# One lasting tile for P1's sums and the results, and ScalarE's last stores behind its last copy, in a convolution and hardswish kernel

## The chip, the cores and the metric

The kernel runs on one core of one Trainium2 chip. Its engines are TensorE (PE in the profile; its weight loads, which overlap the matmuls, are PEld), VectorE (DVE), ScalarE (ACT), GpSimd (POOL) and SyncE (SP), which here only issues transfers. The metric is the device time of one execution in microseconds (us). Beside a run's time the profile has its span, the time from the first to the last instruction of the program.

## The reference

Each head of a lightweight convolution has a softmax over seven taps; the result goes through a feed-forward layer with a hardswish. Cut to what matters:

```python
w = exp(weight - max); w = w / (sum(w) + 1e-9)        # weight [8, 7]
attn[b, s] = sum_k w[head, k] * x_padded[b, s + k]     # x [8, 4096, 192], causal, 24 channels a head
x = attn.reshape(32768, 192)
h = x @ w_in                                           # w_in [192, 2048]
g = h * clip(h + 3.0, 0.0, 6.0) / 6.0
return g @ w_out                                       # w_out [2048, 192], float32
```

## The kernel before

The 32768 tokens are worked through in 32 blocks of 1024 (two groups of N = 512 tokens). Tokens lie along the free dimension, and the 2048 hidden units are 2 x 8 chunks of 128 partitions (`NP` = 8). The first block is computed in a plain way (`out_direct`). Blocks 1 to 31 each go through `first_layer` and `second_layer`. The whole order of instructions is written out by hand: the program is traced under `tc.manual_schedule()`, and each engine runs its instructions in that order. The Tile layer adds the waits that the data need.

**First layer** (`first_layer`). It runs 16 steps, n = 0 to 15. Each step has 18 matmuls (L508) in parts of high and low precision into two PSUM banks, a scaling on ScalarE (L520), the clipped factor on ScalarE (`relu`, L302) and its product with h on VectorE (`gate`, L306), which writes two quarters of the tile `g`. Only after the gate are the banks free for a later step, so a late gate makes TensorE wait. Between the steps stand jobs: before step 0 the results left over from the block before and one tap of the next block's convolution, and after steps 1, 5 and 9 one more tap each (`conv_jobs`, L986, VectorE, 128 x 1536 values, both inputs in SBUF).

Behind each odd step below 8 GpSimd forms **P1's sums** for one pair of chunks: `small_sums` (L575) makes four sums or differences of quarters of A11 and writes them into the tile `s1`, pairs (0, 1), (2, 3), (4, 5), (6, 7) behind steps 1, 3, 5 and 7. Behind the odd steps above 8 it forms S3 (`g_sums`, L412) and issues a transfer that adds A22 onto A21 in place (L556).

**Second layer** (`second_layer`). `g @ w_out` is done by seven products of 2 x 2 blocks (`prod`), a part of each again by seven products of half size (`small`, `level_two`). Matmuls (L616) come in four streams side by side, each with a cost and a due time; `do(t, ...)` puts other engines' work between them. The small products of product 1 read `s1` and are done by clock 32; `tiles` at clock 33 then takes a new tile of results. Its eight chunks of 512 values have these uses:

| chunk | before | after |
|---|---|---|
| 0, 1, 2 | p7, p5, u3 | the same |
| 3 | transposed results on their way out | free in most blocks; fourth buffer in the last |
| 4, 5 | transposed results | the same |
| 6 | p2, and c12 in the last block | the same |
| 7 | fourth buffer in the last block | transposed results |

`store` (L462 and `store_rows`, L372) takes the next chunk from the list `xts`, transposes a result of 96 x 512 values into it on VectorE, and issues three transfers to `out`, one for each 32 rows, on SyncE unless other queues are named. A block has four stores: p7, p2, then u3 and p5, which are finished (`finish`, L837 and the adds at L456) in the next block before step 0.

**The tile's reuse.** `s1` and `results` are tiles of the same pool, one buffer and one tag (`shared`), so they take turns in the same memory. The first instruction that writes a new one waits until everything that read or wrote the old one is done, the transfers to `out` among them. It stands between steps 1 and 2:

```python
if n == 1:
    s1.append(ot.tile([P, NP, N], F32, name="s1", tag="shared")[:])
if n < NP and n % 2:
    small_sums(s1[-1], A11, (1, 2, 3, 4), nc.gpsimd, every[n - 1 : n + 1])
```

**The last block** finishes its own results. `end_lower` makes c12 and u3 for the lower 256 tokens and stores them, rows 0 and 2 of three issued by SyncE and row 1 by ScalarE (`both`). `end_upper` copies the last piece out of PSUM on ScalarE (L825), adds it to c12 on VectorE and to u3 on GpSimd (L827), transposes and stores the upper tokens, rows by SyncE and ScalarE again.

Of the kernel before, what the change touches and what calls it, by code (L numbers as in the profile page):

```python
# [11 lines left out]
F32 = mybir.dt.float32  # L12
# [13 lines left out]
def kernel(  # L26
# [8 lines left out]
    nc = tc.nc  # L35
    P = nc.NUM_PARTITIONS
# [6 lines left out]
    N = 512  # L43
# [11 lines left out]
    NP = NC // 2  # L55
# [8 lines left out]
    ot = ctx.enter_context(tc.tile_pool(name="ot", bufs=1))  # L64
# [55 lines left out]
    w_s = cst.tile([P, 3, 4, NP // 2, QS], F32, name="w_s")  # L120
# [153 lines left out]
    A11, A21, A12, A22 = (g4[:, :, j] for j in range(4))  # L274
# [26 lines left out]
    def relu(r6, h):  # L301
        nc.scalar.activation(r6, h, ACT.Relu, bias=half[:], scale=1.0 / 6.0)  # L302

    def gate(g_, h):

        nc.vector.scalar_tensor_tensor(  # L306
            out=g_, in0=g_, scalar=1.0, in1=h, op0=ALU.min, op1=ALU.mult
        )
# [46 lines left out]
    every = range(NP)  # L355

    results, xts = [], []

    def new_results():
        results[:] = [ot.tile([P, NP, N], F32, name="results", tag="shared")]  # L360
        xts[:] = range(3, 6)

    def next_xt():
        xts.append(xts.pop(0))
        return results[0][:, xts[-1]]

    new_results()

    def store_rows(i, k, q, xt, j, dma=nc.sync, tokens=slice(0, N)):

        t0 = i * TB + k * N
        dma.dma_start(  # L372
            out=out[t0 + tokens.start : t0 + tokens.stop, q * QS : (q + 1) * QS].rearrange("(t r) d -> r t d", r=QS),
            in_=xt[j * QS : (j + 1) * QS, tokens].rearrange("r (t d) -> r t d", d=QS),
        )
# [79 lines left out]
    def add(out, x, y, op=ALU.add):  # L455
        nc.vector.tensor_tensor(out=out, in0=x, in1=y, op=op)  # L456

    def store(i, c, k, half_, qs=range(NQ), queues=(nc.sync,), tokens=slice(0, N)):

        xt = next_xt()  # L460
        r = slice(qs[0] * QS, (qs[-1] + 1) * QS)
        nc.vector.transpose(out=xt[r, tokens], in_=c[r, tokens])  # L462
        for q in qs:
            store_rows(i, k, half_ * NQ + q, xt, q, queues[q % len(queues)], tokens)
# [5 lines left out]
    def r32(ap):  # L470
        return ap.bitcast(F32R)
# [13 lines left out]
        nc.scalar.mul(r32(mix), mix, -4096.0)  # L485

    free_slots = list(range(4))
    y_own, y_other, pools, s1 = [], [None], [], []

    def swap_parts(dma=nc.sync):  # L490
        y_other[0] = pools[0].tile([P, 3, K3, N], F32, name="y_other", tag="other")
# [4 lines left out]
    def first_layer(i, jobs):  # L496

        slots = {}

        def both(n):  # L500
            return psum[:, 2 * slots[n] : 2 * slots[n] + 2]

        def mms(n, part, start=False, stop=False):
            group, c = divmod(n, NP)
            for s in range(K3):
                for k in range(2):
                    r = slice(k * D2, (k + 1) * D2)
                    nc.tensor.matmul(  # L508
                        out=psum[:, 2 * slots[n] + k], lhsT=r32(w_in_parts[part][r, c, s]),
                        rhs=r32(y_other[0][r, part, s] if group else y_own[part][r, s]),  # L510
                        start=start and s == 0, stop=stop and s == K3 - 1,
                        skip_group_check=True,
                    )

        def begin(n):
            slots[n] = free_slots.pop(0)
            mms(n, HIGH, start=True)
            mms(n, LOW)
            if n + 1 < count:
                nc.scalar.mul(both(n), both(n), 4097.0)  # L520
            else:
                lower, upper = (psum[:, 2 * slots[n] + k] for k in range(2))
                nc.scalar.mul(lower, lower, 4097.0)
                nc.vector.tensor_scalar(
                    out=upper, in0=upper, scalar1=4097.0, scalar2=None, op0=ALU.mult
                )

        def end(n):
            group, c = divmod(n, NP)
            mms(n, MIX, stop=True)  # L530
            to = g4[:, c, 1:3] if group else g4[:, c, 0::3]
            relu(to, both(n))
            gate(to, both(n))
            free_slots.append(slots[n])

        count = 2 * NP
        begin(0)
        begin(1)
        for job in jobs.get(-1, ()):
            job()  # L540
        for n in range(count):
            if n == count - 3:
                begin(n + 2)
            end(n)
            if n < count - 3:
                begin(n + 2)
            for job in jobs.get(n, ()):
                job()
            if n == 1:
                s1.append(ot.tile([P, NP, N], F32, name="s1", tag="shared")[:])  # L550
            if n < NP and n % 2:
                small_sums(s1[-1], A11, (1, 2, 3, 4), nc.gpsimd, every[n - 1 : n + 1])
            if n > NP and n % 2:
                pair = slice(n - NP - 1, n - NP + 1)
                g_sums(nc.gpsimd if n + 3 < count else nc.vector, (3,), range(NP)[pair], 2)
                nc.gpsimd.dma_start(out=S1[:, pair], in_=A22[:, pair], accum_op=ALU.add)  # L556
# [7 lines left out]
    def small_sums(to, x, which, engine=nc.gpsimd, r=every):  # L564

        r = slice(r[0], r[-1] + 1)
        x11, x12, x21, x22 = four_parts(x[:, r])
        s1, s2, s3, s4 = four_parts(to[:, r])
        forms = {
            1: (s1, x21, x22, ALU.add), 2: (s2, s1, x11, ALU.subtract),  # L570
            3: (s3, x11, x21, ALU.subtract), 4: (s4, x12, s2, ALU.subtract),
        }
        for n in which:
            o, p, q, op = forms[n]
            engine.tensor_tensor(out=o, in0=p, in1=q, op=op)  # L575
# [10 lines left out]
    def second_layer(i, between):  # L586
# [4 lines left out]
        sums2, p1 = z[:, 0:NP], z[0:DH, NP]  # L591
        ends = [psum[:, 2 * free_slots[0] + k] for k in range(2)] if last else [b, b]
        s5 = A22
        copy = nc.scalar.copy
        m = slice(0, DH)
        lo, hi = halves
        both = nc.sync, nc.scalar
# [39 lines left out]
        def small(n, m_, out, start=False, j=3):  # L637

            x, w = prod[n]
            sums, ws = {  # L640
                1: (s1[-1], w_s[:, 0]), 5: (s5, w_s[:, 1]), 2: (sums2, w_s[:, 2]),
            }[n]
            x11, x12, x21, x22 = four_parts(x)
            z1, z2, z3, z4 = four_parts(sums)
            b11, b12, b21, b22 = (
                w_out[:, h::2, w, q * QS : (q + 1) * QS] for h in range(2) for q in range(2)
            )
            t1, t2, t3, t4 = (ws[:, k] for k in range(4))
            xm, wm = {
                1: (x11, b11), 2: (x12, b21), 3: (z4, b22), 4: (x22, t4),  # L650
                5: (z1, t1), 6: (z2, t2), 7: (z3, t3),
            }[m_]
            for u in range(NP // 2):
                put(j, 1, lambda u=u: matmul(
                    j, out, wm[:, u], xm[:, u], start and u == 0
                ))
# [9 lines left out]
        def tiles():  # L666
            new_results()
            if last:
                xts.insert(0, NP - 1)
            late.update(zip(("p7", "p5", "u3"), (results[0][m, n] for n in range(3))))  # L670
            late["p2"] = results[0][m, 6]

# [128 lines left out]
        def finish(k):  # L801
# [4 lines left out]
                add(p5, b[m], p5)  # L806
            store(i, u3 if k else p5, k, 1)

        def end_lower():
            p5, u3, c12 = late["p5"], late["u3"], results[0][m, 6]  # L810
            two = slice(0, 2 * QS)
            copy(out=p5[third, lo], in_=a[fourth, lo])
            copy(out=c12[third, hi], in_=b[third, hi])
            nc.gpsimd.tensor_tensor(out=u3[two, hi], in0=u3[two, hi], in1=p5[two, hi], op=ALU.add)
            add(c12[two, hi], b[two, hi], p5[two, hi])
            nc.gpsimd.tensor_tensor(out=u3[:, lo], in0=u3[:, lo], in1=p5[:, lo], op=ALU.add)
            store(i, u3, 1, 1, (0, 1), (nc.gpsimd,), hi)
            add(c12[:, lo], b[m, lo], p5[:, lo])
            add(c12[:, lo], ends[0][m, lo], c12[:, lo])
            store(i, c12, 0, 1, queues=both, tokens=lo)  # L820
            store(i, u3, 1, 1, queues=both, tokens=lo)

        def end_upper():
            p5, u3, c12 = late["p5"], late["u3"], results[0][m, 6]
            copy(out=p5[third, hi], in_=c[fourth, hi])  # L825
            add(c12[:, hi], ends[1][m, hi], c12[:, hi])
            nc.gpsimd.tensor_tensor(  # L827
                out=u3[third, hi], in0=u3[third, hi], in1=p5[third, hi], op=ALU.add
            )
            add(c12[third, hi], c[fourth, hi], c12[third, hi])  # L830
            store(i, c12, 0, 1, queues=both, tokens=hi)
            store(i, u3, 1, 1, (2,), (nc.scalar,), hi)
# [33 lines left out]
    with tc.manual_schedule():  # L866
# [82 lines left out]
        n = 3  # L949
# [137 lines left out]
```

## Time and profile before

| | |
|---|---|
| time, median of 3 runs | 2218.27 us (2216.13, 2218.27, 2218.99) |
| profiled execution | 2217.5 us, its span 2215.7 us |
| granted TensorE clock | 0.999 |
| bytes moved by transfers | 264.28 MB, mean 119 GB/s |
| from and to HBM | 31.72 MB read, 25.17 MB written |
| L575 on POOL, 128 x 256 (min / median / max) | 726 to 732 / 739 to 742 / 2251 to 2346 ns |
| L986 on DVE, 128 x 1536, in 186 taps | 1771 / 1814 / 2425 ns |
| transfers of results, issue to landing | 1.5 / 4.3 / 13.7 us |

The page gives busy times of the engines and the chain that ended last: from the last instruction back, at each step, to what released it. In the tables of waits a line has the waiting engine and line, what ended the wait, the sum of the waits in us, their number and the longest. In a timeline a line has the start in us from the span's start, the length, engine, line, operation, what is written and read, how many instructions were merged, and in brackets the idle time before it and what ended that. "ACTq" and "SPq" are the queues of ScalarE and SyncE, where transfers are issued. A busy TensorE is a modelled time, so the chain, not the busy share, tells where it waits.

### The profile page before, as it was taken

What the parts mean: (1) busy time and instruction counts of PE and PEld (TensorE: products, weight loads), DVE (VectorE), ACT (ScalarE), POOL (GpSimd) and SP (SyncE); (2) the same over time, 40 slices, a digit from 0 to 9 for tenths busy, and PEclk for the clock granted to TensorE, in tenths of its full rate; (3) what the DMA queues carried; (4) which work ended last, traced back from release to release, by engine and by line L of the source; (5) the groups of instructions that cost most, each with busy time, mean ns of one, the idle gap of its engine ahead of it and who ended that gap; (6) DMA issues with size and microseconds to landing.
All of it is one profiled execution on the core that took longest, in us unless ns stands there. A gap on an engine that the chain in (4) does not pass through costs nothing.

```text
span 2215.7 us, 53039 instructions
## 1 busy us (share of the span) xinstructions
PE 2208.0 (100%) x22364; PEld 1581.8 (71%) x22364; DVE 1900.8 (86%) x1766; ACT 1615.0 (73%) x2112; POOL 1021.9 (46%) x1029
## 2 busy tenths in 40 slices
PE   9999999999999999999999999999999999999998
PEld 5477777777777777777777777777777777777776
DVE  8888888888898888888888888888888888888876
ACT  7478776687766777767877668776677776687765
POOL 2454543554434555335454355453455543554434
PEclk9999999999999999999999999999999999999999
DMA  6265658656577556685665766666755667656575
GB/s 157 56 116 112 130 106 148 116 109 125 112 133 139 103 109 124 121 149 104 114 125 111 141 124 109 118 119 126 142 101 110 127 114 148 111 111 127 99 134 91
DMA packets 304190, 264.28 MB, mean 119 GB/s; under 512 B 210992, under 2 KB 216112, under 8 KB 303952
## 3 DMA queue, kind: packets, MB, share of 16 engines
q0 software_dynamic: 82240, 201.95, 48.5%
q1 hardware_dynamic: 220472, 58.67, 14.7%
q8 instruction: 175, 2.87, 0.5%
q14 instruction: 63, 0.52, 0.1%
q10 hardware_dynamic: 1240, 0.27, 0.1%
HBM read 31.72 MB, written 25.17 MB: 26 GB/s over the span
## 4 chain that ended last, share of the span: by engine, by line
PE 98%; ACT 1%; DVE 0%; DMA 0%; issue 0%; DVEq 0%; ACTq 0%
PE psum L616 48%; PE psum L508 45%; PE psum L296 2%; PE psum L341 2%; DMA s<-g 0%; PE psum L881 0%; ACT g L302 0%; PE psum L889 0%; ACT psum L520 0%; ACT s L678 0%; DVE g L306 0%; DVE y L986 0%; DVE results L456 0%; DVE results L462 0%; ACT results L791 0%
## 5 line engine op out<-in xcount | busy, mean ns | idle before, releaser
L616 PE MATMUL psum<-g,w_out 128*32 128x512 f32 (+1 forms) x6340 | 899.5, 525 | 0.0
L306 DVE SCALAR_TENSOR_TENSOR g<-g,psum 128x1024 f32<-128x1024 f32 (+1 forms) x528 | 616.5, 1183 | 181.8 <-ACT g L302 181.4
L302 ACT ACTIVATE g<-psum,half 128x1024 f32<-128x1024 f32 (+1 forms) x528 | 564.7, 1086 | 6.3 <-PE psum L508 5.5
L616 PEld LDWEIGHTS psum<-g,w_out 128*32 128x32 f32 x6340 | 389.5, 110 | 217.6 <-issue 102.8
L508 PE MATMUL psum<-y,w_in 64*128 64x512 f32 x4464 | 521.4, 388 | 0.0
L508 PE MATMUL psum<-y_other,w_in 64*128 64x512 f32 x4464 | 519.0, 387 | 0.1
L520 ACT ACTIVATE psum<-psum 128x1024 f32<-128x1024 f32 x465 | 469.0, 1009 | 53.7 <-PE psum L508 50.8
L616 PE MATMUL psum<-s,w_out 128*32 128x512 f32 (+1 forms) x3272 | 503.7, 570 | 0.1
L508 PEld LDWEIGHTS psum<-y,w_in 64*128 64x128 f32 x4464 | 413.5, 184 | 115.7 <-issue 26.0
L508 PEld LDWEIGHTS psum<-y_other,w_in 64*128 64x128 f32 x4464 | 416.9, 184 | 92.1 <-DVE g L306 4.9
L575 POOL TENSOR_TENSOR s<-g 128x256 f32<-128x256 f32 x248 | 228.9, 923 | 426.7 <-DMA out_dram<-results 422.6
L986 DVE SCALAR_TENSOR_TENSOR y<-x,c_sb,y 128x1536 f32<-128x1536 f32 x186 | 346.0, 1860 | 2.6 <-ACT y L984 1.3
L679 POOL DMA_DIRECT2D s<-g x124 | 148.5, 1202 | 335.5 <-ACT s L678 293.0
L616 PE MATMUL psum<-g,w_s 128*32 128x256 f32 x1488 | 285.5, 379 | 0.0
L616 PEld LDWEIGHTS psum<-s,w_out 128*32 128x32 f32 x3272 | 176.4, 110 | 60.1 <-issue 33.0
L556 POOL DMA_DIRECT2D g<-g x124 | 150.0, 1214 | 106.5 <-issue 63.7
L616 PEld LDWEIGHTS psum<-g,w_s 128*32 128x32 f32 x1488 | 159.2, 110 | 42.6
L613 ACT COPY psum<-psum 32x512 f32<-32x512 f32 x186 | 89.4, 481 | 112.7 <-PE psum L616 109.3
L616 PE MATMUL psum<-s,w_s 128*32 128x256 f32 x744 | 170.7, 379 | 0.0
L616 PE MATMUL psum<-z,w_s 128*32 128x256 f32 x744 | 170.6, 379 | 0.0
L412 POOL TENSOR_TENSOR s<-g 128x1024 f32<-128x1024 f32 x62 | 166.8, 2691 | 0.8 <-DVE g L306 0.8
L575 DVE TENSOR_TENSOR g<-g 128x1024 f32<-128x1024 f32 x124 | 146.3, 1221 | 11.7 <-PE psum L616 8.5
(109 smaller groups left out, 2144.4 us busy)
## 6 DMA issues: line engine op xcount, KB each, us to landing
y_other<-y POOLq DMA_DIRECT2D x180, 384.0 KB, 8.8
g<-g POOLq DMA_DIRECT2D x124, 512.0 KB, 5.9
s<-g POOLq DMA_DIRECT2D x124, 512.0 KB, 6.6
out_dram<-results SPq DMA_DIRECT2D x378, 64.0 KB, 4.3
x<-in_x_dram SPq DMA_DIRECT2D x53, 388.5 KB, 5.8
stage<-in_moe_w_in_dram SPq DMA_DIRECT2D x16, 192.0 KB, 4.5
stage<-in_moe_w_out_dram SPq DMA_DIRECT2D x8, 384.0 KB, 6.4
x<-in_x_dram SPq DMA_DIRECT2D x7, 384.0 KB, 4.7
```

The source lines that it names most:

```text
L296: nc.tensor.matmul(out=psum[:, b], lhsT=w[r], rhs=src, start=start, stop=stop, skip_group_check=onto,)
L302: nc.scalar.activation(r6, h, ACT.Relu, bias=half[:], scale=1.0 / 6.0)
L306: nc.vector.scalar_tensor_tensor(out=g_, in0=g_, scalar=1.0, in1=h, op0=ALU.min, op1=ALU.mult)
L412: engine.tensor_tensor(out=o[:, r], in0=a[:, r], in1=b[:, r], op=op)
L508: nc.tensor.matmul(out=psum[:, 2 * slots[n] + k], lhsT=r32(w_in_parts[part][r, c, s]), rhs=r32(y_other[0][r, part, s] if group else y_own[ ...
L520: nc.scalar.mul(both(n), both(n), 4097.0)
L556: nc.gpsimd.dma_start(out=S1[:, pair], in_=A22[:, pair], accum_op=ALU.add)
L575: engine.tensor_tensor(out=o, in0=p, in1=q, op=op)
L613: streams[3].append((t - 0.5, lambda: fn(*args, **kw)))
L616: nc.tensor.matmul(out=out, lhsT=w, rhs=x, start=start, stop=True, tile_position=(0, j * QS), skip_group_check=True,)
L679: nc.gpsimd.dma_start(out=S3[:, pair], in_=A12[:, pair], accum_op=ALU.add)
L986: jobs.append(lambda k=k: nc.vector.scalar_tensor_tensor(out=y[:], in0=x[:, :, k : k + N], scalar=c_sb[:, k : k + 1], in1=y[:], op0=ALU.mu ...
```

## The change

P1's sums and the results get one tile, `shared`, taken once before the loop and never given back. Nothing waits for the tile's release any more; each instruction waits for the earlier readers and writers of the chunk that it writes. The transposed results move from chunks 3, 4, 5 to 4, 5, 7, and the fourth buffer of the last block from 7 to 3. In the last block, ScalarE's two store issues for the lower tokens are kept in a list and issued behind the copy L825.

```diff
+    shared = ot.tile([P, NP, N], F32, name="shared")
+
     def new_results():
-        results[:] = [ot.tile([P, NP, N], F32, name="results", tag="shared")]
-        xts[:] = range(3, 6)
+        results[:] = [shared]
+        xts[:] = 4, 5, 7
...
-            if n == 1:
-                s1.append(ot.tile([P, NP, N], F32, name="s1", tag="shared")[:])
             if n < NP and n % 2:
-                small_sums(s1[-1], A11, (1, 2, 3, 4), nc.gpsimd, every[n - 1 : n + 1])
+                small_sums(shared, A11, (1, 2, 3, 4), nc.gpsimd, every[n - 1 : n + 1])
...
-                1: (s1[-1], w_s[:, 0]), 5: (s5, w_s[:, 1]), 2: (sums2, w_s[:, 2]),
+                1: (shared, w_s[:, 0]), 5: (s5, w_s[:, 1]), 2: (sums2, w_s[:, 2]),
...
             if last:
-                xts.insert(0, NP - 1)
+                xts.insert(0, 3)
...
+        class Later:
+            def dma_start(self, **kw):
+                waiting.append(kw)
+
+        waiting = []
+
         def end_lower():
...
-            store(i, c12, 0, 1, queues=both, tokens=lo)
-            store(i, u3, 1, 1, queues=both, tokens=lo)
+            store(i, c12, 0, 1, queues=(nc.sync, Later()), tokens=lo)
+            store(i, u3, 1, 1, queues=(nc.sync, Later()), tokens=lo)
 
         def end_upper():
             p5, u3, c12 = late["p5"], late["u3"], results[0][m, 6]
             copy(out=p5[third, hi], in_=c[fourth, hi])
+            for kw in waiting:
+                nc.scalar.dma_start(**kw)
             add(c12[:, hi], ends[1][m, hi], c12[:, hi])
```

More of the change, by code (lines that the diff above doesn't have):

```diff
@@ L487 @@
     free_slots = list(range(4))
-    y_own, y_other, pools, s1 = [], [None], [], []
+    y_own, y_other, pools = [], [None], []
     def swap_parts(dma=nc.sync):
```

## The prediction

> **What bounds the kernel now.** I read the page first: the busy shares and the chain of work that ended last.
>
> ```profile
> span 2215.7 us, 53039 instructions
> PE 2208.0 (100%) x22364; PEld 1581.8 (71%) x22364; DVE 1900.8 (86%) x1766; ACT 1615.0 (73%) x2112; POOL 1021.9 (46%) x1029
> ...
> PE 98%; ACT 1%; DVE 0%; DMA 0%; issue 0%; DVEq 0%; ACTq 0%
> ```
>
> TensorE is the bound. Nothing that the change does alters a matmul, so it can gain only where TensorE waits, and after its last matmul. Where it waits is read from the chain of waits in order of time (start, length, what). Two token blocks of it, and a stretch inside the second:
>
> ```profile
> 1869.16 32.91 PE psum L508 x288
> 1902.07 35.04 PE psum L616 x255
> 1937.11 2.97 PE psum L508 x24
> ...
> 1952.40 1.22 DVE g L306
> 1953.62 2.34 DVE y L986
> 1955.96 1.14 DVE g L306
> ...
> 1957.15 13.23 PE psum L508 x114
> 1970.38 35.04 PE psum L616 x256
> ```
>
> A quiet block is 32.91 us of first layer and 35.04 us of second, 67.95 us. The second layer is 35.04 us in every block but the last. The first layer is not: from 1937.11 to 1970.38 it takes 33.27 us, 0.36 more, and there the chain leaves TensorE for a gate (L306), a convolution tap (L986) and the next gate. Over all blocks: the first L508 stage starts at 99.91, the thirty-first at 2141.40. 2041.49 less 30 x 67.95 (2038.50) is 2.99 us. **That 3.0 us is all that first-layer stalls cost.**
>
> Why the tap is late, from the timelines of VectorE (DVE) and GpSimd (POOL) there (start, length, idle before and what ended it):
>
> ```profile
> 1950.70 0.74 POOL L575 TENSOR_TENSOR s<-g 128x256 f32<-128x256 f32 x1 [14.24 <-DMA out_dram<-results]
> ...
> 1953.54 2.42 DVE L986 SCALAR_TENSOR_TENSOR y<-x,c_sb,y 128x1536 f32<-128x1536 f32 x1
> 1953.61 0.73 POOL L575 TENSOR_TENSOR s<-g 128x256 f32<-128x256 f32 x1
> ```
>
> POOL waits 14.24 us for stores to land, starts P1's sums 13.6 us into the stage instead of behind the second gate, and is in the middle of them when the tap of step 5 starts. The tap takes 2.42 us, where an undisturbed one takes 1.81. I compared that tap over the blocks: in all 19 stages over 32.92 us it (in two early blocks the next one, step 9) takes 1.99 us or longer, in the quiet stages 1.81 to 1.98. The list of waits gives the same wait in total:
>
> ```profile
> POOL s L575 <- DMA out_dram<-results: 422.6, 30, 14.5
> ```
>
> **Part 1, one lasting tile.** Removed: the wait of the first sum for everything that ever read `results`. Added: waits by chunk. Pair (0, 1) waits for VectorE's transposes of p7 and p5, which end 4.0 us into the stage, and for gate 1, at 8.5. Pair (2, 3): transpose of u3, gate 3 (12.5). Pair (4, 5): the stores from chunks 4 and 5, and gate 5 (16.6). POOL's wait for all stores together ended 8.5 to 14.0 us into the stage in every block, so the gate comes last. Pair (6, 7): chunk 7's store and gate 7 (20.7). Queued behind the sums on POOL are S3 (L412) and the accumulating transfers (L556); they can only come earlier.
>
> The trace has a block in which POOL is not held up, the first of the thirty-one, at 99.91. Its POOL and DVE timelines are my template:
>
> ```profile
> 108.18 1.81 DVE L986 SCALAR_TENSOR_TENSOR y<-x,c_sb,y 128x1536 f32<-128x1536 f32 x1
> ...
> 114.97 0.75 POOL L575 TENSOR_TENSOR s<-g,s 128x256 f32<-128x256 f32 x1
> 116.50 2.25 POOL L575 TENSOR_TENSOR s<-g 128x256 f32<-128x256 f32 x1 [0.79 <-DVE g L306]
> ...
> 123.13 0.74 POOL L575 TENSOR_TENSOR s<-g,s 128x256 f32<-128x256 f32 x1
> ```
>
> Here the sums of each pair wait for the gate that the tap follows directly on VectorE. The tap therefore starts first (108.18, 116.34, 124.50, each 1.81 us) and the sum gives way (2.25 us for 0.74). Both intervals in which POOL could be in the middle of a sum end in time: 114.97 + 0.75 = 115.72, 0.62 before the tap at 116.34; 123.13 + 0.74 = 123.87, 0.63 before 124.50. The stage is 32.91 us. L412 begins 24.8 us into the stage instead of 28.4, the first two L556 2.1 us earlier. That pulls their transfers forward, into a stretch where the swaps (landed by 10.9 us) are over; the second layer of this first block is 35.04 us with them there. So the 3.0 us go, and nothing new is late. Bounds: 0 (the stalls stay) to -3.0. I take -3.0, since the template's gates and taps stand within 0.2 us of the other blocks'. More waits for POOL's sequencer are hidden: its semaphore reads take some 0.04 us each, and six of them are 0.25, under the 0.62 of slack.
>
> The writes into `shared` that follow in the second layer (L702 on) waited for P1's last matmul before and wait for the same matmuls, chunk by chunk, now: 0. Other chunk numbers for transposed results: four buffers in the last block before and after, 0.
>
> **Part 2, the last block's stores.** The timeline of the end, and SyncE's waits in the last 15 us:
>
> ```profile
> 2209.51 0.88 ACTq L372 DMA_DIRECT2D out_dram<-results  x2
> 2209.73 0.42 DVE L456 TENSOR_TENSOR results<-psum,results 96x256 f32<-96x256 f32 x1
> 2210.43 0.36 ACT L825 COPY results<-psum 32x256 f32<-32x256 f32 x1 [3.00 <-DVE results L456]
> 2210.83 0.43 DVE L456 TENSOR_TENSOR results<-psum,results 32x256 f32<-32x256 f32 x1 [0.68 <-ACT results L825]
> ...
> SPq L372 <- DMA out_dram<-results: 1.0, 1, 1.0
> ```
>
> ScalarE's copy L825 stands behind two store issues (0.88 us). VectorE's add at 2209.73 started as the matmuls ended, so the copy, alone, could run at 2209.76 to 2210.12. VectorE's next add then starts when its own former one is done, 2210.15 + 0.04 = 2210.19, not 2210.83: 0.64 sooner. Both transposes behind it, POOL's add L827 and ScalarE's upper stores follow by 0.64. Past the copy go two issues: they now stand at 2210.16 to 2211.04, just before the first upper store is ready at about 2211.1, so they hold up nothing on ScalarE; their data lands 0.65 us later, at 2212.6 and 2213.0 (they took 2.4 us).
>
> The end is SyncE's. It finished the lower issues at 2211.34, then waited 1.0 us for the landing of an earlier store (by the times, ScalarE's second, landed 2212.31) and issued its two upper stores at 2212.37 and 2212.73; the last landed at 2214.44, 1.7 us on. Which store it waits for after the change, the trace of before can't show. None: issues at 2211.38 and 2211.74, end at 2213.45, -1.0 us. One of SyncE's own lower stores (2211.8 to 2212.1): -0.5. ScalarE's first: +0.3. ScalarE's second, as now: 2213.0, then 2213.4 + 1.7 = 2215.1, +0.7. I take the middle, -0.1, and keep -1.0 to +0.7.
>
> **The sum.** The profiled execution took 2217.5 us, span 2215.7 and 1.8 around it: 2217.5 - 3.0 - 0.1 = 2214.4. It lay 0.8 under the median of the runs shown, 2218.27. I don't add the 0.8: second layers and quiet first layers repeat to 0.02 us, so I take the spread between runs to be in the stalls themselves.
>
> **The rivals.**
>
> *The tail in full.* Part 1 as above and SyncE's wait gone: 2217.5 - 3.0 - 1.0 = 2213.5. For it: 1.0 us of waiting stands there. Against: every upper store still follows ten lower and earlier ones, two of which now land later.
>
> *Half the stalls stay.* POOL still meets taps in some blocks, where a store lands late or a sum slips: 2217.5 - 1.5 = 2216.0. For it: blocks 3 and 5 of thirty-one lost 0.3 us at step 9, where another phase of POOL met the tap. Against: the template.
>
> *Slower: a sum in flight at every tap.* If POOL reaches the fourth sum of pair (2, 3) 0.62 us later than the template, it is in flight when the tap of step 5 starts, in every block instead of some. The stalled stages lose 0.16 us on the mean (3.0 / 19) and 0.36 at most. Thirty times that, on the stall-free 2214.4, is 2219.2 to 2225.2. For it: the sums move to a place where they pass three taps, not two, and the template's block swapped halves from another queue. Against: gates set the starts, and 0.62 us is most of a sum.
> The Trainium skill, page "SBUF — State Buffer", section "Who interferes with whom", says that a VectorE instruction with two SBUF inputs and a GpSimd instruction that reads SBUF contend for one port pair, and that the one issued second waits for all of the other. Both orders in this trace agree (2.42 against 1.81 us, 2.25 against 0.74); by that rule alone a move of sums towards taps is a risk, and this rival is what it would cost.
>
> *It doesn't do what it says.* If the first sum still waits for all chunks, POOL starts 13.6 us into the stage as now: 2217.5, give or take the tail. Against: before, the transposes into one chunk of `results` ran while stores from others were on their way.
>
> **How the numbers follow.** Forecast 0.52, tail in full 0.20, half the stalls 0.14, slower 0.08, no effect 0.06. A measurement of this kernel tells 0.2%, 4.4 us, from no change: the border is 2213.8. The forecast's own range, 2213.2 to 2215.6 (the tail's bounds, and runs that spread by over 1 us), crosses it; I give 0.45 of it to faster, and nine tenths of the full tail: 0.23 + 0.18, about 0.42. Slower is 0.08, the rest, 0.50, within. The range, 2212.4 to 2217.8, leaves out the slower rival and the edges of the others, some 0.15.
>
> **What would show it.** Right: POOL's wait for `out_dram<-results` gone from the list of waits, or under 20 us in total; the first sum some 8.5 us into each stage; the tap of step 5 at 1.81 us; all first-layer stages at 32.9; thirty blocks in 2038.5 us; the copy L825 within 0.1 us of the last matmul's end. Wrong: taps over 2.0 us with POOL early (the contention moved), second-layer stages off 35.04 (something of POOL's earlier transfers collides), or a last landing over 4.7 us after the last matmul's end, which is what it is now, 2214.44 - 2209.75 (SyncE's wait grew).

## The result and the profile after

| | before | after |
|---|---|---|
| median, us | 2218.44 (2216.01 to 2219.17, 22 runs) | 2214.19 (2213.87 to 2214.58, 22 runs) |
| ratio of the times | | 0.9982, 95% interval 0.9976 to 0.9989 |
| profiled execution, us | 2217.5 (span 2215.7) | 2214.33 (span 2212.6) |
| thirty blocks, first L508/L510 stage to the thirty-first | 2041.49 | 2038.94 |
| last matmul's end to the end of the span | 6.04 | 5.48 |

The change made the kernel 4.25 us faster, 0.19%: just within the 0.2% that the prediction drew as its border, while the interval of the ratio leaves no change out. The predicted 2214.4 is 0.2 us off. The runs also lie closer together: 0.7 us apart where they were 3.2 apart.

Line numbers after the change: L510 is the matmul of the first layer (L508 before), L994 the tap (L986), L374, L458 and L464 the stores, adds and transposes, L831 the last copy (L825), L835 GpSimd's add (L827), L414 the sum S3 (L412), L522 ScalarE's scaling (L520) and L833 the issue of the transfers that were kept back. Kernels with lines put in count on from there.

The busy shares of after, and the last line of its chain of work that ended last:

```profile
span 2212.6 us, 53012 instructions
PE 2205.5 (100%) x22364; PEld 1619.9 (73%) x22364; DVE 1888.4 (85%) x1766; ACT 1613.6 (73%) x2112; POOL 1070.3 (48%) x1029
...
PE 99%; DVE 0%; DMA 0%; SPq 0%; ACT 0%; issue 0%; DVEq 0%; ACTq 0%
```

VectorE is busy 12.4 us less (1900.8 before), 10.5 of it in the taps: no tap of steps 5 and 9 is stretched any more. GpSimd is busy 48 us more (1021.9 before). P1's sums have little part in that (454.2 us before, 457.9 after), since they gave way to taps before, too. 43 us are in S3 (GpSimd forms it behind steps 9 and 11, VectorE behind 13 and 15): the first in each stage now starts 0.16 us behind the tap of step 9 and takes 3.9 us, the second 2.9. S3's rows on the two pages:

```profile
L412 POOL TENSOR_TENSOR s<-g 128x1024 f32<-128x1024 f32 x62 | 166.8, 2691 | 0.8 <-DVE g L306 0.8
```

```profile
L414 POOL TENSOR_TENSOR s<-g 128x1024 f32<-128x1024 f32 x62 | 209.4, 3377 | 24.8 <-DVE g L306 24.7
```

The longer S3 costs TensorE nothing: the second layers behind it take 35.04 us, as before. The chain in order of time, over the two blocks shown before:

```profile
1866.97 32.91 PE psum L510 x288
1899.88 35.04 PE psum L616 x256
1934.92 32.98 PE psum L510 x288
1967.90 35.04 PE psum L616 x256
```

The stage that took 33.27 us takes 32.98, and the chain no longer leaves TensorE for gate, tap and gate. GpSimd's waits (first line), its timeline in that stage, and VectorE's tap of step 5:

```profile
POOL shared L575 <- DVE g L306: 301.9, 64, 9.4
```

```profile
1943.69 2.24 POOL L575 TENSOR_TENSOR shared<-g 128x256 f32<-128x256 f32 x1 [9.44 <-DVE g L306]
...
1950.33 0.74 POOL L575 TENSOR_TENSOR shared<-g,shared 128x256 f32<-128x256 f32 x1
1951.58 2.25 POOL L575 TENSOR_TENSOR shared<-g 128x256 f32<-128x256 f32 x1 [0.51 <-DVE g L306]
```

```profile
1951.42 1.81 DVE L994 SCALAR_TENSOR_TENSOR y<-x,c_sb,y 128x1536 f32<-128x1536 f32 x1
```

The 422.6 us of waiting for `out_dram<-results` are gone; what GpSimd waits for is the gate. The first sum starts 8.8 us into the stage (1943.69 less 1934.92), was 13.6. The fourth sum of pair (2, 3) ends at 1951.07, 0.35 before the tap; the tap takes 1.81 us, and the next sum, started 0.16 behind it, takes 2.25. (In the other stages it ends 0.56 to 0.63 before the tap. In this one a scaling on ScalarE starts 3.34 us into the stage, in the one before 3.07, and the gates and sums follow it.) All 30 taps of step 5 and all 30 of step 9 are at 1.81 us, where step 5 had a median of 2.05 and reached 2.42.

The end, from the timeline and SyncE's waits:

```profile
2207.12 0.95 DVE L458 TENSOR_TENSOR shared<-psum,shared 96x256 f32<-96x256 f32 x2
2207.16 0.36 ACT L831 COPY shared<-psum 32x256 f32<-32x256 f32 x1 [2.34 <-PE psum L616]
2207.22 0.92 ACTq L833 DMA_DIRECT2D out_dram<-shared  x2
2207.67 0.71 POOL L835 TENSOR_TENSOR shared<-shared 32x256 f32<-32x256 f32 x1 [0.53 <-ACT shared L831]
2208.58 0.82 ACTq L374 DMA_DIRECT2D out_dram<-shared  x2
...
2209.22 0.81 SPq L374 DMA_DIRECT2D out_dram<-shared  x2
```

```profile
SPq L374 <- DMA out_dram<-shared: 0.4, 1, 0.4
```

The last matmul releases VectorE and ScalarE at 2207.14 (2209.75 before), 0.07 us behind the end of its row, from which the table above counts; times "after the last matmul" are counted from this release. The copy starts 0.02 us behind it. The two transfers written behind it are issued from 2207.22 on, 0.06 us after the copy has *started*: ScalarE's queue issues them while the copy runs, and doesn't wait for its end at 2207.52. They land at 2209.15 and 2209.53. SyncE still waits for a landing, 0.4 us in place of 1.0, and issues its first upper store 2.08 us after the last matmul, where it was 2.62. The kept traces show which landing it waits for: each issue has a semaphore on which its landing counts, and SyncE's first upper store has semaphore 107, which in before is that of ScalarE's second lower store (landed 2212.31) and in after that of ScalarE's first (2209.15).

**The account** of the profiled pair, 3.17 us (2217.5 less 2214.33): 2.55 in the thirty blocks, 0.56 behind the last matmul, 0.06 in the rest. The thirty blocks of after stand 0.44 over thirty of 67.95 us (2038.50). Less rounded, a quiet block is 67.947 us (26 in a row in `late_two` below, from 168.00 to 1934.61), thirty are 2038.40, and after stands 0.54 over them: in 12 of the thirty the first layer is longer without any long tap, 11 times by 0.04 to 0.07 us and once by 0.02. The stage of 32.98 above is the longest of them.

### The profile page after: what moved, and what is told of

Read it like the earlier page. It is cut to its first block, busy times and chain, and to the rows that moved or that the text cites. A ratio compares the mean times of both kernels' runs of the same rounds, so it can differ in the third digit from the quotient of the medians.

```text
span 2212.6 us, 53012 instructions
## 1 busy us (share of the span) xinstructions
PE 2205.5 (100%) x22364; PEld 1619.9 (73%) x22364; DVE 1888.4 (85%) x1766; ACT 1613.6 (73%) x2112; POOL 1070.3 (48%) x1029
## 4 chain that ended last, share of the span: by engine, by line
PE 99%; DVE 0%; DMA 0%; SPq 0%; ACT 0%; issue 0%; DVEq 0%; ACTq 0%
PE psum L616 49%; PE psum L510 46%; PE psum L296 2%; PE psum L341 2%; DMA x<-in_x_dram 0%; DVE shared L458 0%; DVE shared L464 0%; SPq L100 0%; SPq L133 0%; DVE top L175 0%; PE psum L889 0%; DVE y L255 0%; SPq L89 0%; ACT y L903 0%; ACT scale L186 0%
## 5 line engine op out<-in xcount | busy, mean ns | idle before, releaser
L510 PE MATMUL psum<-y,w_in 64*128 64x512 f32 x4464 | 522.2, 388 | 0.0
L510 PE MATMUL psum<-y_other,w_in 64*128 64x512 f32 x4464 | 516.6, 386 | 0.0
L522 ACT ACTIVATE psum<-psum 128x1024 f32<-128x1024 f32 x465 | 469.0, 1009 | 51.1 <-PE psum L510 48.8
L510 PEld LDWEIGHTS psum<-y,w_in 64*128 64x128 f32 x4464 | 429.0, 184 | 100.8 <-issue 26.0
L510 PEld LDWEIGHTS psum<-y_other,w_in 64*128 64x128 f32 x4464 | 438.9, 184 | 67.0
L575 POOL TENSOR_TENSOR shared<-g 128x256 f32<-128x256 f32 x248 | 273.9, 1105 | 301.9 <-DVE g L306 301.9
L994 DVE SCALAR_TENSOR_TENSOR y<-x,c_sb,y 128x1536 f32<-128x1536 f32 x186 | 335.5, 1804 | 2.6 <-ACT y L992 1.4
L414 POOL TENSOR_TENSOR s<-g 128x1024 f32<-128x1024 f32 x62 | 209.4, 3377 | 24.8 <-DVE g L306 24.7
L616 PEld LDWEIGHTS psum<-s,w_out 128*32 128x32 f32 x3024 | 156.2, 110 | 53.3 <-issue 32.9
L616 PE MATMUL psum<-shared,w_s 128*32 128x256 f32 x744 | 170.7, 379 | 0.0
L575 DVE TENSOR_TENSOR g<-g 128x1024 f32<-128x1024 f32 x124 | 146.4, 1222 | 17.6 <-PE psum L616 14.4
```

What stands on the lines that cost most here:

```text
L414: engine.tensor_tensor(out=o[:, r], in0=a[:, r], in1=b[:, r], op=op)
L510: nc.tensor.matmul(out=psum[:, 2 * slots[n] + k], lhsT=r32(w_in_parts[part][r, c, s]), rhs=r32(y_other[0][r, part, s] if group else y_own[ ...
L616: nc.tensor.matmul(out=out, lhsT=w, rhs=x, start=start, stop=True, tile_position=(0, j * QS), skip_group_check=True,)
L994: jobs.append(lambda k=k: nc.vector.scalar_tensor_tensor(out=y[:], in0=x[:, :, k : k + N], scalar=c_sb[:, k : k + 1], in1=y[:], op0=ALU.mu ...
```

## The experiments

The theory: the 3 us sat in the stalls at the taps of step 5, made by sums of GpSimd in flight there, and part 1 removes them; part 2 gives a little at the end. All kernels were timed beside the kernel before on the same chip; three groups ran on three chips, with before at 2216.17, 2219.02 and 2218.59, so kernels of one group are compared with each other.

**Part 1 alone: `p1_only`, and `p1_again` in the third group.** The stores of the lower half stay as they were:

```diff
-            store(i, c12, 0, 1, queues=(nc.sync, Later()), tokens=lo)
-            store(i, u3, 1, 1, queues=(nc.sync, Later()), tokens=lo)
+            store(i, c12, 0, 1, queues=both, tokens=lo)
+            store(i, u3, 1, 1, queues=both, tokens=lo)
```

> Part 1 alone: the lasting tile and the new chunks, ScalarE's lower stores ahead of its copy as before. Theory (POOL early, so no tap meets a sum): first-layer stages within 0.1 us of 32.9, thirty blocks in 2038.5 to 2039.0 us, all of the after's gain but the last 0.6 us: 2.5 to 3.6 us under before, and the end stays 6.0 us behind the last matmul. Rival (the tail gave most of it): less than 1 us under before.

Measured: 2214.21 us (2213.68 to 2215.78), ratio 0.9990 (0.9982 to 0.9999). That is 1.96 under before, where 2.5 to 3.6 were expected; before itself took 2216.17 in this group, 2.3 less than in the result. The taps, minimum / median / maximum in ns, and SyncE's wait at the end:

```profile
L994 DVE SCALAR_TENSOR_TENSOR y<-x,c_sb,y x186: 1771/1812/2010, 76.5 to 2096.4; 128x1536 f32<-128x1536 f32 x186
```

```profile
SPq L374 <- DMA out_dram<-shared: 0.9, 1, 0.9
```

No tap near 2.4 us is left (the 2010 is in the first of the stages, and stands in after too), and the end is before's: last matmul to end 5.98. Its thirty blocks took 2039.78, over the 2039.0 expected and 1.4 over the quiet ones, with 0.047 us more in nearly every first-layer stage and no long tap. The profiled run, 2215.78, was the slowest of the eleven; the others took 2213.68 to 2214.46.

> Part 1 alone again, now beside the whole change on one chip, so that part 2 shows without the scatter of the stalls. Theory (part 2 is worth the 0.5 to 0.6 us that the profiles show between the last matmul and the end): 0.5 to 0.7 us slower than after_third. Rival (what ends a run behind the profiled instructions hides it): within 0.2 us of after_third.

`p1_again` took 2215.69 (2215.47 to 2215.81), beside it `after_third`, the changed kernel once more, 2215.05 (2214.67 to 2215.25). Last matmul to end is 6.05 against 5.47. So part 2 is worth 0.64 us by the medians and 0.58 by the profiles.

> The changed kernel once more, to be compared with the two others on the same chip. Every theory: 2213.9 to 2215.2 us.

Its profile has thirty blocks of 2039.83, again with the 0.047 us in nearly every stage.

**Part 2 alone: `p2_only`.** Tiles and chunks as before:

```diff
-    shared = ot.tile([P, NP, N], F32, name="shared")
...
-        results[:] = [shared]
-        xts[:] = 4, 5, 7
+        results[:] = [ot.tile([P, NP, N], F32, name="results", tag="shared")]
+        xts[:] = range(3, 6)
...
+            if n == 1:
+                s1.append(ot.tile([P, NP, N], F32, name="s1", tag="shared")[:])
...
```

> Part 2 alone: ScalarE's two lower stores behind its copy, the tiles in turn as before. Theory: first-layer stages stalled as before (thirty blocks 2041 to 2042 us), 0.4 to 0.8 us less between the last matmul and the end: 0.4 to 0.8 us under before, if the scatter of the stalls lets it be seen. Rival (the tail gave most): 2 us or more under before.

Measured: 2216.97 (2214.96 to 2218.76), ratio 1.0002 (0.9993 to 1.0010): 0.80 over before by the medians, and no difference by the interval. The list of waits and the taps:

```profile
POOL s L575 <- DMA out_dram<-results: 407.6, 29, 14.5
```

```profile
L994 DVE SCALAR_TENSOR_TENSOR y<-x,c_sb,y x186: 1771/1814/2424, 76.5 to 2100.1; 128x1536 f32<-128x1536 f32 x186
```

GpSimd's wait and the taps up to 2.42 us are back, and the end is the new one, 5.45 us. The thirty blocks took 2043.58, more than the 2041 to 2042 expected: 5.2 over the quiet ones, of which the 0.047 us of each stage are 1.4 and the stalls 3.8. The 0.6 us of the end can't be seen in the time, since this kernel's runs differ by 3.8 us. In the profiles the two parts act in two places: each of these two kernels has its own part's effect, and before's behaviour in the other place.

**Are the chunks needed? `chunks_345`.** The lasting tile, but with the results in their old places, so that pair (2, 3) writes into a chunk whose store may still be on its way:

```diff
-        xts[:] = 4, 5, 7
+        xts[:] = 3, 4, 5
...
-                xts.insert(0, 3)
+                xts.insert(0, NP - 1)
```

> The lasting tile with the old chunks 3, 4, 5 for transposed results (fourth buffer 7). Theory: pair (2, 3) writes chunk 3 and must wait for the store of p5 out of it, which lands 8 to 14 us into the stage; its sums then run to 12 to 17 us and are in flight at the tap of step 5 (16.5 us) in some blocks; POOL's wait for transfers to out comes back with 100 to 200 us in total, and 0.5 to 2.5 us of the gain are lost: 2214.7 to 2216.7 us. Rival (what counts is that no release of a whole tile is waited for; the chunks don't matter): 2214.2 us.

Measured: 2213.61 (2213.19 to 2215.42), ratio 0.9989 (0.9980 to 0.9997). My theory of a wait there fell. GpSimd's sums wait for a store once, 1.1 us in the last block, where no tap follows, and in no other stage; the taps stay at 1.81. The first write into chunk 3 in a stage that starts at 508.29 (chain, then GpSimd's timeline):

```profile
508.29 32.95 PE psum L510 x288
```

```profile
522.01 0.74 POOL L575 TENSOR_TENSOR shared<-shared,g 128x256 f32<-128x256 f32 x1
```

It comes 13.7 us into the stage, and the wait for all stores together had ended 8.5 to 14.0 us in: this store has landed by then. It is close: in the stages behind the first, the last landing of results that the trace has lies 10.9 to 13.5 us into the stage. What paid was that waits go by chunk; moving the chunks was not needed, by 0.2 us in the closest of these stages.

**The slower rival: `late_two` and `late_mid`.** The rival said that a sum in flight at every tap of step 5 would cost 0.16 to 0.36 us a stage. `late_two` makes GpSimd do two sums again behind pair (2, 3), to push one into the tap:

```diff
                 small_sums(shared, A11, (1, 2, 3, 4), nc.gpsimd, every[n - 1 : n + 1])
+                if n == 3:
+                    for _ in range(2):
+                        small_sums(shared, A11, (1,), nc.gpsimd, every[2:4])
```

> After, with the first sum of pair (2, 3) formed two times more behind that pair in every block (the same values are written again; 1.4 us of work for POOL). Theory: the second extra sum is in flight when the tap of step 5 starts at 16.5 us, the tap takes 2.1 to 2.5 us in every block, each of 30 stages loses 0.1 to 0.36 us: 3 to 11 us slower than after, 2217 to 2225 us. Rival (the gain came from fewer waits, not from where the sums stand; POOL is far from its bound): 2214.2 us.

Measured: 2213.55 (2213.27 to 2213.74), ratio 0.9987 (0.9978 to 0.9996): no slower than its neighbours in the group (`chunks_345` 2213.61, `p1_only` 2214.21). The two extra sums (L578 is L575 of after) and the tap between their starts (L997 is L994), in one stage:

```profile
1338.91 0.74 POOL L578 TENSOR_TENSOR shared<-g 128x256 f32<-128x256 f32 x1
...
1339.73 2.21 POOL L578 TENSOR_TENSOR shared<-g 128x256 f32<-128x256 f32 x1
```

```profile
1339.53 1.81 DVE L997 SCALAR_TENSOR_TENSOR y<-x,c_sb,y 128x1536 f32<-128x1536 f32 x1
```

A sum *was* in flight when the tap started, the first of the extra two: it ended at 1339.65, 0.12 behind the start. The second, started 0.20 behind the tap, gave way. The tap still took 1.81 us, and so it is in 29 of the 30 blocks; in one a sum ends 0.33 us into the tap, which takes 1.95. The expectation missed because the extra sums came later than it had them, and a sum that ends 0.12 us into the tap costs it nothing. In the thirty blocks of before, the taps of steps 5 and 9 that such a sum stretches follow 1.81 + (end of the sum, counted from the tap's start, - 0.20) us to 0.01 us. `late_mid` was made from that law, with a sum of half the size first, so that the whole one ends 0.6 us into the tap:

```diff
+                if n == 3:
+                    nc.gpsimd.tensor_tensor(
+                        out=shared[:, 2, 0:128], in0=A11[:, 2, 256:384], in1=A11[:, 3, 256:384], op=ALU.add
+                    )
+                    small_sums(shared, A11, (1,), nc.gpsimd, every[2:4])
```

> After, with two more sums behind pair (2, 3) in every block (values are written again): one of half the size, which ends near 16.3 us, and a whole one, which then runs from 16.3 to 17.1 us. The tap of step 5 starts at 16.50. Theory (a tap waits for the sum in flight; by the 30 blocks of before its length is 1.81 us plus what the sum runs beyond 0.20 us after the tap's start, and TensorE loses 0.1 us at a tap of 2.15 and 0.2 us at 2.25): taps of step 5 at 2.1 to 2.3 us in every block, 0.08 to 0.21 us lost in each of 30 stages, 2.4 to 6.3 us slower than after. Rival (where the sums stand doesn't matter, fewer waits on POOL made the gain): as after_again, within 0.3 us.

Measured: 2220.94 (2220.74 to 2221.32), against 2215.05 (2213.99 to 2215.16) for the changed kernel in the same group, `after_again`: 5.9 us slower. GpSimd (L554 is the sum of half the size, L580 is L575 of after), the tap (L999) and the stage:

```profile
1343.25 0.46 POOL L554 TENSOR_TENSOR shared<-g 128x128 f32<-128x128 f32 x1
1343.79 0.74 POOL L580 TENSOR_TENSOR shared<-g 128x256 f32<-128x256 f32 x1
```

```profile
1343.89 2.25 DVE L999 SCALAR_TENSOR_TENSOR y<-x,c_sb,y 128x1536 f32<-128x1536 f32 x1
```

```profile
1327.41 33.18 PE psum L510 x288
```

The sum ends at 1344.53, 0.64 into the tap; the law gives 1.81 + 0.64 - 0.20 = 2.25, and 2.25 it is. 29 of 30 taps of step 5 took 2.24 to 2.26 us (in the other the whole sum started behind the tap and gave way, and the tap took 1.81), the thirty blocks 2045.69. Over the 2039.83 of `after_third`, whose stages carry the same 0.047, that is 5.9 us, 0.20 for each of the 29. `late_two` is the control: it has two extra sums in each block as well, and more work in them, but in all blocks except one the sum in flight ends within 0.13 us of the tap's start, and nothing is lost (thirty blocks 2038.48). So the claimed cause of the stalls is turned on and off by where a sum ends.

> The changed kernel itself, to be compared with the two others on the same chip. Every theory: 2213.9 to 2214.6 us.

In the profile of `after_again` the thirty blocks took 2038.54 us, 0.14 over the quiet ones. This run, 2213.99, was the fastest of the eleven. The other ten took 2214.96 to 2215.16, so the median lies over the 2213.9 to 2214.6 expected; 0.047 us in each stage would be about that much, but none of the ten was traced.

**What is left at the end: `pool_store` and `pool_late`.** If ScalarE's and SyncE's queues set the end, one of the six stores of the lower tokens could go to GpSimd. `pool_store` lets it issue one row of u3's as soon as it is ready:

```diff
-            store(i, u3, 1, 1, queues=(nc.sync, Later()), tokens=lo)
+            store(i, u3, 1, 1, queues=(nc.sync, Later(), nc.gpsimd), tokens=lo)
```

> After, with row 2 of u3's lower store issued by GpSimd instead of SyncE. Theory (the end is SyncE's: it issues the upper stores of c12 late, since it is busy with its own lower ones and waits for the landing of ScalarE's): SyncE has one issue of 0.46 us less, its first upper store meets no wait for a landing and goes out 0.5 to 0.7 us sooner, the second still waits for ScalarE's first lower store and goes out 0.3 to 0.4 us sooner; the end comes 0.3 to 0.4 us sooner after the last matmul. Rival (the end is ScalarE's own upper stores or POOL's add, which GpSimd's issue of 0.6 us pushes back): no gain, or up to 0.2 us lost.

Measured: 2214.88 (2214.71 to 2215.05) against 2215.05 for `after_again`; last matmul to end 5.27 against 5.50. GpSimd's end:

```profile
2208.26 0.58 POOL L374 DMA_DIRECT2D out_dram<-shared  x1 [0.34 <-DVE shared L464]
...
2208.90 0.72 POOL L835 TENSOR_TENSOR shared<-shared 32x256 f32<-32x256 f32 x1
```

Of the 0.3 to 0.4 us, 0.2 came in the profile, and the 0.17 in the time is less than such runs differ by. The rival was half right: the issue pushes the add L835 back to 0.99 us after the last matmul (0.53 in after), and with it ScalarE's upper store, which now lands last. `pool_late` therefore issues that row behind the add:

```diff
-            store(i, u3, 1, 1, queues=(nc.sync, Later()), tokens=lo)
+            store(i, u3, 1, 1, queues=(nc.sync, Later(waiting), Later(behind_pool)), tokens=lo)
...
+            for kw in behind_pool:
+                nc.gpsimd.dma_start(**kw)
             add(c12[third, hi], c[fourth, hi], c12[third, hi])
```

> After, with row 2 of u3's lower store issued by GpSimd behind its last add L827 (L835 in after) instead of by SyncE. Theory (the end is SyncE's queue and its wait for a landing; in pool_store it became GpSimd's add, held up by the issue ahead of it): GpSimd's add is where it is in after, ScalarE's last upper store too; SyncE's second upper store goes out 0.3 to 0.4 us sooner; the last landing comes 0.3 us sooner than in after, 5.1 to 5.3 us from the last matmul to the end (5.5 in after). Rival (GpSimd's store, issued 1.3 us after the last matmul, lands last, as its issue takes 0.6 and its landing 2.4 us): 5.5 us or more.

Measured: 2215.45 (2215.01 to 2215.84), 0.40 slower than `after_third`, last matmul to end 5.86 and not 5.1 to 5.3. The stores land a little sooner, the last one 4.01 us after the last matmul (4.13 in after), and GpSimd's own is not the last. What ends the run is something that neither side had named: GpSimd's closing drain, an instruction on its queue at the end of the program. Its longest in ns, in `pool_late` and then in after:

```profile
L1095 POOLq DRAIN  x3: 46/93/3976, 2209.2 to 2213.7; - x3
```

```profile
L1090 POOLq DRAIN  x3: 46/102/2960, 2207.6 to 2212.3; - x3
```

In after it lasts from 2207.64 to 2210.60, and SyncE's last landing (2211.27) is behind it. In `pool_late` it lasts to 2213.19, 3.24 us after GpSimd's issue ended, and the last landing (2212.18) lies before it. No version tried is clearly faster than the changed kernel.

## Why the prediction was right, point by point

**Part 1, "I take -3.0".** Right, with the mechanism shown: stalls gone with the part alone (`p1_only`), back without it (`p2_only`), and made again by one sum in flight (`late_mid`). The profiled pair gained 2.55. By the unrounded quiet block the stalls had cost 3.09 us, not 2.99, and 0.54 of it came back in the stages that are up to 0.07 us longer without a long tap, which the prediction didn't have; an execution with quiet stages (`after_again`, 2038.54) gains 2.95. The template held: first sum 8.5 to 8.8 us into the stage, taps at 1.81, second layers at 35.04.

**Part 2, "I take the middle, -0.1".** The right sign, mis-sized: -0.56 in the profile, -0.64 by the medians of `p1_again` and `after_third`. (`p1_only` against `chunks_345` and `late_two`, 2214.21 against 2213.6, says the same, but those two differ from the changed kernel in other ways, too.) The step that failed is "they now stand at 2210.16 to 2211.04 ... their data lands 0.65 us later". The issues were set behind the end of the copy, and they go out while it runs. And they took 1.9 and 1.8 us to land, not 2.4. Counted from the last matmul, the landings were worked out as 2.85 and 3.25 us later and came at 2.01 and 2.39. Of the first's 0.84 us, 0.33 is the earlier issue and 0.5 the shorter way to landing; why that was shorter these runs don't show. SyncE did wait for ScalarE's first store, the case priced at +0.3, and with these terms it became a gain. The row that could have warned is in the same timeline: before, the two issues at 2209.51 (0.88 us) stand ahead of ScalarE's copy, which starts behind them; nothing in it says whether an issue behind a copy waits for the copy's end. Both cases should have been among the bounds. They were wide enough (-1.0 to +0.7), so the sum held: -3.0 - 0.1 forecast, -2.55 - 0.56 found. The two errors cancel, and that is luck: in the quiet execution of `after_again` the same kernel took 2213.99.

**"I don't add the 0.8."** This came out: after's runs spread over 0.7 us, and their median lies 0.14 from the profiled execution. The reason was right in part. Without stalls a second spread is left, as in the eleven runs of `p1_only` (ten within 0.8 us, one 1.3 above them), and the changed kernel's median was 2215.05 in both other groups. So it is in part luck that the median met the forecast to 0.2 us.

**The slower rival.** Its price was right (0.20 us a stage for a tap of 2.25). Its point was wrong: "0.62 us later" would not have been enough. A sum may run 0.20 us past the tap's start for nothing, and 0.12 past it cost nothing in `late_two`. The prediction's own example, the tap of 2.42, is not one of a sum in flight: its sum starts at 1953.61, 0.07 behind the tap (1953.54), and still goes first. Two more sums in before, started 0.03 and 0.04 us behind the tap of step 9, did so, too (taps of 2.38 and 2.39); another 0.07 behind gave way, like those 0.16 and 0.20 behind. The rule in the Trainium skill, page "SBUF — State Buffer", section "Who interferes with whom", that whoever issues first has the shared ports for its whole instruction and the other waits, agrees with the 2.25 for 0.74; in the other order these runs show the wait less 0.20 us, and by the starts in the trace the three sums just behind a tap don't fit it.

**The other rivals.** The tail in full: SyncE's wait went from 1.0 to 0.4, not to nothing. Half the stalls, and no effect: the taps of step 5 and 9 exclude both.

## What to carry to other kernels

When one engine's long wait ends at a fixed place, look at whose work it then collides with: here a wait of 14 us on an engine with half its time free cost TensorE only through the 0.7 us sum that it put next to a tap. A tile that two uses take in turns makes the first writer wait for the slowest reader of all parts; one lasting tile, with the same order of work, lets each part wait for its own. At the end of a program price an issue by when its queue can send it, not by the end of the instruction written ahead of it, and count every engine's closing drain.

## What the runs showed of the hardware that was not expected

- A tap (two inputs in SBUF) is delayed only by what the GpSimd sum runs on beyond 0.20 us of the tap's start: 0.12 us into it, 1.81; 0.33, 1.95; 0.64, 2.25. A sum that starts up to 0.07 us behind the tap can still go first (2.42 in before). GpSimd's issues of transfers (L266, L267), running as a tap of the same shape starts, hardly delay it: 1.77 and 1.82 us.
- ScalarE's queue issued a transfer 0.06 us after the start of a copy of 0.36 us that stood ahead of it.
- GpSimd's drain at the end of `pool_late` lasted 3.24 us beyond its last issue, where that transfer had landed 1.6 us behind the issue (2211.54). In after, where an add comes last, it ended 2.2 us behind the add.
- In some executions nearly every first-layer stage is 0.047 us longer (1.4 us in thirty blocks), in others hardly any, of the same kernel (`after_third` 2039.83, `after_again` 2038.54). The taps are 1.81 us in both. In the profile of after, which has stages of both kinds, the matmuls of a longer one fall behind 3.1 to 5.4 us into the stage, before any of P1's sums. The cause stays open.
